# A fused adaLN block, forward and gradients: row loads on POOL's queue, three turns on TensorE, LN and gate work per 128 tokens

## The chip, the core and the metric

The kernel runs on one core of one Trainium2 chip. The metric is device time in microseconds of one execution. Engines are named as in the profile: PE (TensorE matmul), PEld (its weight loads), DVE (VectorE), ACT (ScalarE), POOL (GpSimd), SP (SyncE, here only a queue that issues DMAs).

## The reference

The forward pass is an adaLN-modulated transformer block on one sequence of 2048 tokens, D = 512, 32 heads of 16, and a feed-forward width of 1792 with a squared ReLU. The kernel returns its output and the gradients of nine inputs for a given `grad_out`, all in bfloat16.

```python
mod = (silu(c) @ w_mod).reshape(1, 6, 1, 512)
sa, ca, ga, sb, cb, gb = (mod[:, i] for i in range(6))
h = layernorm(x) * (1 + ca) + sa
q, k, v = split_heads(h @ wqkv)                  # 32 heads of 16
p = softmax(einsum('bhqd,bhkd->bhqk', q, k) * 16 ** -0.5)
x = x + ga * (merge(p @ v) @ wo)
h = layernorm(x) * (1 + cb) + sb
r = relu(h @ w1 + b1)
out = x + gb * ((r * r) @ w2 + b2)
# returned: out and d(out . grad_out)/d(x, wqkv, wo, w1, b1, w2, b2, c, w_mod)
```

## The kernel before

**Four stretches.** A preparation makes LN1, the first keys, queries and values. Then comes the forward attention, with most of the feed-forward and its gradients woven in. Then the last chunk of 512 tokens is finished (`last_chunk`), and then the attention's gradient (the loop over `order_t` and `order_n`) and the final products run. The change touches the second stretch alone.

**Units.** The forward attention is 512 units: 4 query chunks of 512 tokens, in each 8 groups of 4 heads, in each 16 key tiles of 128. For unit u, `fscore(u)` lets PE multiply four heads' keys with the queries (L560, 32 rows of PE for each head) into two PSUM tiles `psST` of two banks, and ACT takes the exponential of each into `ET` (L562). There are three such PSUM tiles, so PE can be about a unit and a half ahead of ACT. `fpv(u - 2)` multiplies `ET` with the values into the one bank `oacc` (L576). After a head group's last tile DVE copies `oacc` to `ostage` (L580), POOL casts it to `obf` (L588), and SP turns it by a DMA transpose into `O_un`.

**What else a unit holds.** All other products of this stretch go through one PSUM bank, the tile `pm` of pool `psM` (function `mm()`, one buffer), so PE can begin the next product only when DVE has copied the last one out. The queues for this work are written by hand:

- `plan` says at which unit the remaining projections of queries, keys and values, token tiles and modulation rows run (`plan_tasks`), and `later_stage` does side jobs every fourth unit: among them LN1's modulated rows `h1_st` (L700 to L703).
- `later(lag, f, ...)` puts a call into `due`, which `run_due` empties at the start of each unit; most DMAs on SP's queue are issued so.
- `dense_chunk(c, O_c, L)` is a generator for one chunk of 512 tokens: the attention's output `O_c` turned to `OT`, the projection with `wo` (L347), LN2, its rows turned to `h2T`, two feed-forward products (L398, L412), LN2's gradient (L434 to L467), the second feed-forward product (L487) and the gradient through `wo` (L519). `step(u)` runs it to its next `yield`; `yield k` makes it wait k further units.
- Products over tokens for the weights' gradients are chains in `dwq` (`add_chain`). Each is four matmuls, a copy by DVE into one of four `part` tiles (L251), and a store to `p_st`: SP's for chunk 0, and for later chunks an accumulating DMA issued by POOL (L255). They run where the generator waits. Chunk 2's chains that are left when the units end run inside `last_chunk` (into `dwbuf`).
- Where a unit has no product, `steady` runs two filler matmuls (L599).

**A chunk's start.** Seven units after a query chunk's last head group, `ffinish` scales its heads (L603) and `chunk_loads(c)` issues the chunk's loads of the gradient, `wo` and x (0.5 MB each) and queues the weights' loads. The last chunk has its own path (`early_finish`, `late_finish`, `last_chunk`).

**What the change touches.** `fload` loads the keys (four transfers of 16 rows x 2048) and queries (four of 16 x 512 and one row of bounds per head, `m_st`) of the next head group, all nine on SP's queue in one unit, at key tile 4 of the group before (tile 10 in the first seven groups). `scaled` multiplies a chunk's gradient by the gate `gb` in one POOL instruction of 128x2048; `sums` adds its four tiles to a row sum. Three turns in `dense_chunk` are DMA transposes from SBUF to SBUF on SP's queue, each followed by a wait of several units:

```python
later(3, sp, OT.rearrange("p t o q -> p (t o) q"), flat(O_c), True)
yield 6
...
later(3, sp, h2T.rearrange("p t o q -> p (t o) q"), flat(xn2_c), True)
yield 6
...
later(5, sp, daT.rearrange("p t o q -> p (t o) q"), flat(da_c), True)
w2_nat = load_wB(w2_src, 1, 0.5)
yield 5
```

Of the kernel before, what the change touches and what calls it, by code (L numbers as in the profile page):

```python
# [15 lines left out]
ALU = mybir.AluOpType  # L16
AX = mybir.AxisListType
BF = dt.bfloat16
F32 = dt.float32

P = 128
D = 512
DC = 4
# [11 lines left out]
def kernel(  # L35
# [8 lines left out]
    TT = n // P  # L44
# [102 lines left out]
    with ExitStack() as ph:  # L147
# [142 lines left out]
        def chunk_loads(c):  # L290
            ts = slice(4 * c, 4 * c + 4)
            end = c == QC - 1
            if end:
                L = dict(begun)
            else:
                L = {"w1": load_wA(w1_src, 6), "w1T": load_wB(w1T_st[:], 20)}
                L["g"] = cb.tile([P, 4, D], BF, name="g_c", tag="g_c")
                sp(L["g"][:], g_dram[:, ts, :])
            L["wo"] = ffw.tile([P, DC, D], BF, name="wo_nat", tag="wo")
            sp(L["wo"][:], A_wo.rearrange("(oc p) j -> p oc j", p=P))  # L300
            L["x1"] = cb.tile([P, 4, D], BF, name="x1_c", tag="x1_c")
            sp(L["x1"][:], x_dram[:, ts, :])
            L["gf"] = cb.tile([P, 4, D], BF, name="gf_c", tag="gf")
            L["gfT"] = cb.tile([P, 4, DC, P], BF, name="gfT", tag="gfT")

            def scaled():
                POOL.tensor_tensor(L["gf"][:], L["g"][:], gb_bc.unsqueeze(1).to_broadcast([P, 4, D]), ALU.mult)
                later(6, sp, L["gfT"].rearrange("p t o q -> p (t o) q"), flat(L["gf"]), True)

            def sums():  # L310
                for ti in range(4):
                    rowsum(4, L["g"][:, ti, :], 4 * c + ti)

            if end:
                return L
            later(5, scaled)
            later(16, sums)
            return L

        def dense_chunk(c, O_c, L):  # L320
# [16 lines left out]
            def normed(ti):  # L337
                t = 4 * c + ti
                DVE.tensor_scalar(xn2_c[:, ti, :], x1_c[:, ti, :], mv4[:, ti, 0:1], rstd2[:, t:t + 1], ALU.subtract, ALU.mult)

            OT = cb.tile([P, 4, DC, P], BF, name="OT", tag="T4")
            later(3, sp, OT.rearrange("p t o q -> p (t o) q"), flat(O_c), True)
            yield 6
            for ti in range(4):
                pa = mm()
                for oc in range(DC):
# [9 lines left out]
            rsqrt_cols(wk, rstd2[:, ts], mv4[:, :, 1], 4)  # L356
            for ti in range(4):
                normed(ti)
            later(3, sp, h2T.rearrange("p t o q -> p (t o) q"), flat(xn2_c), True)
            yield 6  # L360
            while dwq and dwq[0][1] < c:
                yield -2
            for ic in range(DC):
                DVE.tensor_scalar(h2T[:, :, ic, :], h2T[:, :, ic, :],
                                  modcol[:, 4, ic:ic + 1], modcol[:, 3, ic:ic + 1], ALU.mult, ALU.add)
                if ic == 1:
                    yield 0

            def h2_tokens():
                while dwq and dwq[0][1] < c:  # L370
# [105 lines left out]
            dwq[0:0] = chains  # L476
            later(5, sp, dx1_st[:, ts, :], dx1_c)
            daT = cb.tile([P, 4, DC, P], BF, name="daT", tag="T4")
            later(5, sp, daT.rearrange("p t o q -> p (t o) q"), flat(da_c), True)

            w2_nat = load_wB(w2_src, 1, 0.5)
            yield 5
            for ti in range(4):
                t = 4 * c + ti
                pf = mm()
# [58 lines left out]
        def fload(qc, hg):  # L544
            i = hg % 2
            kt_sb, qt_sb = kts[i], qts[i]
            load_rows(kt_sb, qkT_st[1], hg, slice(0, n))
            load_rows(qt_sb, qkT_st[0], hg, slice(512 * qc, 512 * qc + 512), m_st)
            fh[qc, hg] = (qt_sb, kt_sb)

        def fscore(u):
# [113 lines left out]
        def later_stage(i):  # L665
            if i < 4:
                vT = tmpT[:, 4 * (i % 2):4 * (i % 2) + 4, :].rearrange("p a q -> p (a q)")
                sp(vT[:, 0:n], v_st[:, i * P:(i + 1) * P], True)
                later(3, sp, vT_st[i * P:(i + 1) * P, :], vT[:, 0:n])
                return  # L670
            if i < 8:
                ic = i - 4
                nat = tmpT[:, 0:2, :]
                sp(nat, A_wqkv[ic * P:(ic + 1) * P, D:].rearrange("p (t d) -> p t d", t=2))
                nat = nat.rearrange("p t (g d) -> p t g d", d=DH)
                vkp = tmpT[:, 8:10, :].rearrange("p a (g v d) -> p (a g) v d", v=2, d=DH)
                POOL.tensor_copy(vkp[:, :, 1, :], nat[:, 0])
                POOL.tensor_copy(vkp[:, :, 0, :], nat[:, 1])
                later(3, sp, wpad_st[ic * P:(ic + 1) * P, :], tmpT[:, 8:10, :].rearrange("p a q -> p (a q)"))
                return  # L680
            if i < 14:
                for j in (2 * (i - 8), 2 * (i - 8) + 1):
                    wT = tmpT[:, j % 8, :]
                    src = A_wqkv[:, j * P:(j + 1) * P] if j < 4 else wpad_st[:, (j - 4) * P:(j - 3) * P]
                    sp(wT, src, True)
                    later(3, sp, wT_st[j], wT)
                return
            if i >= 26:
                return
            if i == 25:  # L690
                for r, j in enumerate((1, 4)):
                    DVE.reciprocal(racc[0:1, r, :], modbc[0:1, j, :])
                later(3, sp, rows_st[6:8, :].unsqueeze(0), racc[0:1, 0:2, :])
                return
            if i in (18, 20, 21, 24):
                g = (18, 20, 21, 24).index(i)
                hr = tmpT[:, 4 * (g % 3):4 * (g % 3) + 4, :]
                for ti in range(4):
                    t = 4 * g + ti
                    DVE.tensor_scalar(hr[:, ti, :], hr[:, ti, :], mean1[:, t:t + 1], rstd1[:, t:t + 1], ALU.subtract, ALU.mult)  # L700
                DVE.tensor_tensor(hr, hr, ca1_bc.unsqueeze(1).to_broadcast([P, 4, D]), ALU.mult)
                DVE.tensor_tensor(hr, hr, sa_bc.unsqueeze(1).to_broadcast([P, 4, D]), ALU.add)
                later(3, sp, h1_st[:, 4 * g:4 * g + 4, :], hr)  # L703
            if i in (14, 15, 16, 22):
                g = (14, 15, 16, 22).index(i)
                sp(tmpT[:, 4 * (g % 3):4 * (g % 3) + 4, :], x_dram[:, 4 * g:4 * g + 4, :])
# [263 lines left out]
        def plan_tasks():  # L970
            R, T = {}, {}

            def at(u, f, *args):
                plan.setdefault(u, []).append((f, args))
# [51 lines left out]
                later(1, sp, m_st[h0:h1, chunk_cols(g)], mrow[h0:h1, :])  # L1026
                yield

            def query_bound(u, g, hbs, rate):
# [5 lines left out]
                for i in range(6):  # L1035
                    at(u + 1 + i // rate, lambda: next(R["g"]))

            def b1_turn():
                pb = pools["mm"].tile([P, 2 * 512], BF, name="pb1", tag="pm")
# [35 lines left out]
            for g in range(QC):  # L1075
# [6 lines left out]
                at(81 + g, token_tile, 0, 3, g)  # L1082
                for ti in range(4):
                    at(85 + 4 * g + ti, token_tile, 1, g, ti)
            query_bound(21, 0, (1,), 2)
            at(22, b1_turn)
            query_bound(41, 0, (2, 3), 1)
            query_bound(50, 1, (0, 1, 2, 3), 1)
            query_bound(66, 2, (0, 1, 2, 3), 1)
            query_bound(80, 3, (0, 1, 2, 3), 1)  # L1090
# [41 lines left out]
        stages = [*range(4, 14), *range(4), 30, 31, *range(14, 26)]  # L1132
        with ExitStack() as ph2:
            pools["s"] = ph2.enter_context(tc.tile_pool(name="psS", bufs=3, space=bass.MemoryType.PSUM))
            pools["o"] = ph2.enter_context(tc.tile_pool(name="psO", bufs=1, space=bass.MemoryType.PSUM))
# [1 line left out]
            with tc.manual_schedule(engines={PE.engine, ACT.engine, DVE.engine, SP.engine, POOL.engine}):  # L1137
                fh[0, 0] = (qts[0], kts[0])
                for u in range(NF + 2):
                    unit[0] = u  # L1140
                    run_due()
                    if u < NF:
                        if funits[u][2] == (10 if u < 7 * TT else 4) and u + TT < NF:
                            fload(*funits[u + TT][0:2])
                        fscore(u)
                    if 2 <= u:
# [858 lines left out]
```

## Time and profile before

| | |
|---|---|
| median of 3 runs | 2506.2 us (2504.3 to 2511.26) |
| the profiled execution, its own time | 2512.69 us |
| its span, first to last instruction | 2510.9 us |
| mean granted TensorE clock | 0.977 |
| ACT busy | 2304.1 us, 92% of the span |
| PE busy | 2336.8 us, 93% |
| DVE busy | 1818.7 us, 72% |
| POOL busy | 348.1 us, 14% |
| DMA, mean rate | 176 GB/s, 442.40 MB |

A line of the profile's groups reads: source line, engine, operation, output tile <- input tiles, shapes, count, busy us, mean ns of one, and then the idle time of the engine just before these instructions and what ended it. Matmul ends are modelled and pipelined, so busy PE is not PE at its peak. In timelines each row is start (us from the span's start), length, engine, line, operation and tiles, count, and in brackets the idle time before it with its releaser. Rows on SPq are DMA issues: their length is the queue's time, not the transfer's.

### The profile page before, as it was taken

The page shows a single profiled execution, that of the slowest core. Times are in us where ns is not written, and L with a number is a line of the kernel's source. Part 1 is how long each engine was busy: PE and PEld are TensorE (multiplying, and loading weights), DVE is VectorE, ACT ScalarE, POOL GpSimd, SP SyncE. Part 2 cuts the span into 40 slices and gives each one's busy share as a digit, 9 for nine tenths or more (in the row PEclk, how much of TensorE's full clock was granted, in tenths as well). Part 3 has the DMA queues.
Part 4 walks back from the last instruction along what each step waited for, and adds up shares of the span by engine and source line. Part 5 has one row for each costly group of instructions (what it writes and reads, how often), then busy time and mean ns, then how long its engine had stood idle before and what let it go on. Part 6 is the DMA issues. An engine that isn't in the chain of part 4 may idle for free.

```text
span 2510.9 us, 49682 instructions
## 1 busy us (share of the span) xinstructions
PE 2336.8 (93%) x18934; PEld 778.5 (31%) x18934; DVE 1818.7 (72%) x2326; ACT 2304.1 (92%) x3563; POOL 348.1 (14%) x373
## 2 busy tenths in 40 slices
PE   8898889989998999999999999999999999999989
PEld 3232223222322332442332323323232332332244
DVE  6555153445435454578999989999999999999965
ACT  7999999999998999638999999999999999999944
POOL 2000000210323142200111101111011110110100
PEclk9999999999999999998999999999999999999999
DMA  4467455356748766979999999999999999999984
GB/s 142 126 173 174 137 131 133 93 160 134 112 85 169 148 121 129 255 227 172 203 197 198 204 204 204 199 201 203 204 199 202 201 206 200 205 201 211 201 252 133
DMA packets 1207477, 442.40 MB, mean 176 GB/s; under 512 B 1083843, under 2 KB 1178497, under 8 KB 1206854
## 3 DMA queue, kind: packets, MB, share of 16 engines
q1 hardware_dynamic: 1179318, 404.37, 81.6%
q0 software_dynamic: 10944, 16.78, 4.8%
q10 hardware_dynamic: 16976, 18.07, 2.8%
q8 instruction: 149, 2.44, 0.4%
q14 instruction: 90, 0.74, 0.1%
HBM read 98.30 MB, written 70.80 MB: 67 GB/s over the span
## 4 chain that ended last, share of the span: by engine, by line
PE 41%; ACT 39%; issue 7%; DVE 7%; DMA 4%; SPq 1%; ACTq 1%; DVEq 0%; POOL 0%; POOLq 0%
ACT E_u L1583 23%; ACT ET L562 12%; PE dqacc L1664 4%; PE psST L560 4%; PE psS_A L1577 3%; PE pm L233 3%; PE accVK L1637 2%; PE oacc L576 2%; PE psS_B L1577 2%; ACT dsT L1743 2%; DMA dsT<-dS_u 2%; PE psS_C L1577 2%; PE pm L398 2%; PE pm L412 2%; PE pdh L1841 2%
## 5 line engine op out<-in xcount | busy, mean ns | idle before, releaser
L1599 DVE TENSOR_TENSOR dS_u<-psD_u,E_u 128x1024 bf16<-128x1024 f32 x1024 | 1185.8, 1218 | 77.3 <-PE psD_u L1597 29.9
L562 ACT ACTIVATE ET<-psST 128x1024 bf16<-128x1024 f32 x1024 | 942.5, 1251 | 27.5 <-PE psST L560 27.2
L1583 ACT ACTIVATE E_u<-psS_A 128x512 bf16<-128x512 f32 x768 | 510.6, 665 | 10.7 <-DMA d_st<-dltT 7.7
L1583 ACT ACTIVATE E_u<-psS_B 128x512 bf16<-128x512 f32 x768 | 503.8, 656 | 12.4 <-DMA dsT<-dS_u 3.3
L1597 PE MATMUL psD_u<-iv,ido 32*128 32x512 bf16 x2048 | 409.3, 388 | 0.2
L560 PE MATMUL psST<-qt_sb,kt_sb 32*128 32x512 bf16 x2048 | 317.5, 389 | 51.6 <-ACT ET L562 46.9
L1583 ACT ACTIVATE E_u<-psS_C 128x512 bf16<-128x512 f32 x512 | 334.5, 653 | 3.4 <-PE psS_B L1577 1.5
L1577 PE MATMUL psS_B<-ik,iq 32*128 32x512 bf16 x768 | 295.6, 385 | 12.4 <-ACT E_u L1583 4.8
L1577 PE MATMUL psS_A<-ik,iq 32*128 32x512 bf16 x768 | 294.1, 383 | 11.4 <-DVE dwlast L237 1.0
L1577 PEld LDWEIGHTS <-iq 32*128 32x128 bf16 x2048 | 130.0, 91 | 315.6 <-issue 299.7
L1637 PE MATMUL accVK<-dS_u,qz 128*32 128x512 bf16 x2048 | 213.2, 390 | 0.5 <-PE psD_u L1597 0.2
L576 PE MATMUL oacc<-ET,vaug 128*32 128x512 bf16 x2048 | 208.2, 397 | 1.9 <-DVE ostage L580 1.9
L1646 PE MATMUL accVK<-E_u,dOs_tok 128*16 128x512 bf16 x2048 | 204.6, 388 | 0.0
L1682 POOL TENSOR_TENSOR dQacc<-dQacc,dqtmp 128x512 f32<-128x512 f32 x64 | 81.2, 1269 | 857.7 <-ACT dqtmp L1677 857.7
L1577 PE MATMUL psS_C<-ik,iq 32*128 32x512 bf16 x512 | 194.4, 380 | 4.7 <-ACT dqtmp L1677 0.2
L560 PEld LDWEIGHTS <-kt_sb 32*128 32x128 bf16 x2048 | 85.7, 91 | 342.1 <-issue 321.5
L1664 PE MATMUL dqacc<-dsT,KS_tok 128*32 128x512 bf16 x2048 | 147.3, 386 | 19.2 <-DMA dsT<-dS_u 4.9
L1743 ACT ACTIVATE dsT<-ptT 128x1024 bf16<-128x1024 bf16 x128 | 144.8, 1131 | 11.5 <-PE ptT L1627 10.7
L251 DVE COPY part<-pm 128x512 f32<-128x512 f32 (+2 forms) x103 | 63.5, 616 | 119.9 <-PE pm L233 108.2
L1597 PEld LDWEIGHTS <-ido 32*128 32x128 bf16 x2048 | 104.4, 91 | 99.5 <-issue 93.5
L1637 PEld LDWEIGHTS <-qz 128*32 128x32 bf16 x2048 | 58.5, 94 | 178.0 <-issue 162.9
L576 PEld LDWEIGHTS <-vaug 128*32 128x32 bf16 x2048 | 53.1, 93 | 121.7 <-issue 121.7
(404 smaller groups left out, 2517.2 us busy)
## 6 DMA issues: line engine op xcount, KB each, us to landing
p_st<-part POOLq DMA_DIRECT2D x36, 256.0 KB, 5.1
kt_sb<-qkT_st SPq DMA_DIRECT2D x124, 64.0 KB
wA<-in_B_w_dram SPq DMA_DIRECT2D x28, 256.0 KB
wB<-w1T_st SPq DMA_DIRECT2D x21, 256.0 KB
wA<-w2T_st SPq DMA_DIRECT2D x21, 256.0 KB
wB<-in_B_w_dram SPq DMA_DIRECT2D x21, 256.0 KB
p_st<-part POOLq DMA_DIRECT2D x25, 192.0 KB, 4.7
p_st<-part SPq DMA_DIRECT2D x18, 256.0 KB
```

Source lines behind the costliest of these rows:

```text
L560: PE.matmul(ps[:, hi, :], kt_sb[r:r + 32, kt * P:(kt + 1) * P], qt_sb[r:r + 32, :], start=True, stop=True, tile_position=(r, 0))
L562: ACT.activation(ET[:, 2 * pair:2 * pair + 2, :], ps[:], AF.Exp, scale=SCALE)
L576: PE.matmul(oacc[32 * hq:32 * hq + 32, :], lhsT, ET[:, hq, :], start=(kt == 0), stop=(kt == TT - 1), tile_position=(0, 32 * hq), skip_grou ...
L1577: PE.matmul(psS[:], st["q"][r:r + 32, qt * P:(qt + 1) * P], st["k"][r:r + 32, kc * 512:kc * 512 + 512], start=True, stop=True, tile_positi ...
L1583: ACT.activation(bst[u][0][:, hq, :], sst.pop((u, hq))[:], AF.Exp, scale=SCALE)
L1597: PE.matmul(psD[:, hi, :], st["do"][r:r + 32, qt * P:(qt + 1) * P], st["v"][r:r + 32, kc * 512:kc * 512 + 512], start=True, stop=True, til ...
L1599: DVE.tensor_tensor(dS_u[:, 2 * pair:2 * pair + 2, :], psD[:], E_u[:, 2 * pair:2 * pair + 2, :], ALU.mult)
L1637: PE.matmul(cur["vk"][32 * hq:32 * hq + 32, :], hst[hg]["qz"][:, qt, hq, :], bst[u][1][:, hq, :], start=(qt == 0), stop=False, tile_positi ...
L1646: PE.matmul(acc[32 * hq:32 * hq + DH, :], dOs_tok[:, qt, (hg * 4 + hq) * DH:(hg * 4 + hq + 1) * DH], E_u[:, hq, :], start=False, stop=(qt ...
L1664: PE.matmul(acc[32 * hq:32 * hq + 32, :], KS_tok[:, kc * 4 + kt, h * DH:h * DH + 32], tT[:, :, hq * 4 + kt, :], start=(kt == 0), stop=(kt ...
L1682: POOL.tensor_tensor(dst2, dst, tmp[:], ALU.add)
L1743: ACT.activation(dst, pt[:], AF.Identity)
```

## The change

- `fload` puts the nine row loads of a head group on POOL's queue, one in each of nine successive units from key tile 4 on (from the first group on).
- `turned(half, src)` transposes two 128-token tiles by eight PE transposes into the `pm` bank; DVE copies `OT` and `daT` out of it, and for `h2T` applies the modulation on the way out. The waits around the turns change: 6, 6 and 5 units become 2, 2 and 2, with a unit for each half, and two further units after daT's second half.
- The gate's product runs on POOL per 128 tokens in four successive units; its row sums come one in every second unit from 24 units after the loads on, instead of four together after 16.
- LN1's rows for `h1_st` are done per 128 tokens in four successive units. Two reciprocals of 1x512 move from side stage 25 (unit 110) to units 130 and 132.
- The first query bound's steps come slightly earlier (`after` lists the units).

```diff
-            def scaled():
-                POOL.tensor_tensor(L["gf"][:], L["g"][:], gb_bc.unsqueeze(1).to_broadcast([P, 4, D]), ALU.mult)
-                later(6, sp, L["gfT"].rearrange("p t o q -> p (t o) q"), flat(L["gf"]), True)
+            def scaled(ti):
+                POOL.tensor_tensor(L["gf"][:, ti, :], L["g"][:, ti, :], gb_bc, ALU.mult)
+                if ti < 3:
+                    return
+                later(3, sp, L["gfT"].rearrange("p t o q -> p (t o) q"), flat(L["gf"]), True)
...
-            later(5, scaled)
-            later(16, sums)
+            for ti in range(4):
+                later(5 + ti, scaled, ti)
+                later(24 + 2 * ti, sums, ti)
...
+            def turned(half, src):
+                products[0] += 1
+                pt = pools["mm"].tile([P, 2, DC, P], BF, name="ptC", tag="pm")
+                for k in range(2):
+                    for oc in range(DC):
+                        PE.transpose(pt[:, k, oc, :], src[:, 2 * half + k, oc * P:(oc + 1) * P], identb[:])
+                return pt
+
             OT = cb.tile([P, 4, DC, P], BF, name="OT", tag="T4")
-            later(3, sp, OT.rearrange("p t o q -> p (t o) q"), flat(O_c), True)
-            yield 6
+            yield 2
+            for half in range(2):
+                DVE.tensor_copy(OT[:, 2 * half:2 * half + 2], turned(half, O_c)[:])
+                yield 0
...
-            later(3, sp, h2T.rearrange("p t o q -> p (t o) q"), flat(xn2_c), True)
-            yield 6
+            yield 2
             while dwq and dwq[0][1] < c:
                 yield -2
-            for ic in range(DC):
-                DVE.tensor_scalar(h2T[:, :, ic, :], h2T[:, :, ic, :],
-                                  modcol[:, 4, ic:ic + 1], modcol[:, 3, ic:ic + 1], ALU.mult, ALU.add)
-                if ic == 1:
-                    yield 0
+            for half in range(2):
+                pt = turned(half, xn2_c)
+                for ic in range(DC):
+                    DVE.tensor_scalar(h2T[:, 2 * half:2 * half + 2, ic, :], pt[:, :, ic, :],
+                                      modcol[:, 4, ic:ic + 1], modcol[:, 3, ic:ic + 1], ALU.mult, ALU.add)
+                yield 0
...
-            later(5, sp, daT.rearrange("p t o q -> p (t o) q"), flat(da_c), True)
-
             w2_nat = load_wB(w2_src, 1, 0.5)
-            yield 5
+            yield 2
+            for half in range(2):
+                DVE.tensor_copy(daT[:, 2 * half:2 * half + 2], turned(half, da_c)[:])
+                yield 2 * half
...
-            load_rows(kt_sb, qkT_st[1], hg, slice(0, n))
-            load_rows(qt_sb, qkT_st[0], hg, slice(512 * qc, 512 * qc + 512), m_st)
+            rows = list(row_loads(kt_sb, qkT_st[1], hg, slice(0, n)))
+            rows += row_loads(qt_sb, qkT_st[0], hg, slice(512 * qc, 512 * qc + 512), m_st)
+            for i, (to, fro) in enumerate(rows):
+                later(i, POOL.dma_start, to, fro)
+            run_due()
...
-                for ti in range(4):
-                    t = 4 * g + ti
-                    DVE.tensor_scalar(hr[:, ti, :], hr[:, ti, :], mean1[:, t:t + 1], rstd1[:, t:t + 1], ALU.subtract, ALU.mult)
-                DVE.tensor_tensor(hr, hr, ca1_bc.unsqueeze(1).to_broadcast([P, 4, D]), ALU.mult)
-                DVE.tensor_tensor(hr, hr, sa_bc.unsqueeze(1).to_broadcast([P, 4, D]), ALU.add)
-                later(3, sp, h1_st[:, 4 * g:4 * g + 4, :], hr)
+
+                def modulated(ti, t):
+                    DVE.tensor_scalar(hr[:, ti, :], hr[:, ti, :], mean1[:, t:t + 1], rstd1[:, t:t + 1], ALU.subtract, ALU.mult)
+                    DVE.tensor_tensor(hr[:, ti, :], hr[:, ti, :], ca1_bc, ALU.mult)
+                    DVE.tensor_tensor(hr[:, ti, :], hr[:, ti, :], sa_bc, ALU.add)
+
+                for ti in range(4):
+                    later(1 + ti, modulated, ti, 4 * g + ti)
+                later(6, sp, h1_st[:, 4 * g:4 * g + 4, :], hr)
...
-            query_bound(21, 0, (1,), 2)
+            query_bound(21, 0, (1,), (1, 1, 1, 2, 2, 3))
...
+            for r, j in enumerate((1, 4)):
+                at(130 + 2 * r, DVE.reciprocal, racc[0:1, r, :], modbc[0:1, j, :])
+            at(134, sp, rows_st[6:8, :].unsqueeze(0), racc[0:1, 0:2, :])
...
-                        if funits[u][2] == (10 if u < 7 * TT else 4) and u + TT < NF:
+                        if funits[u][2] == 4 and u + TT < NF:
```

More of the change, by code (lines that the diff above doesn't have):

```diff
@@ L304, in chunk_loads, with sums @@
             L["gfT"] = cb.tile([P, 4, DC, P], BF, name="gfT", tag="gfT")
-            def scaled():
-                POOL.tensor_tensor(L["gf"][:], L["g"][:], gb_bc.unsqueeze(1).to_broadcast([P, 4, D]), ALU.mult)
-                later(6, sp, L["gfT"].rearrange("p t o q -> p (t o) q"), flat(L["gf"]), True)
-            def sums():
-                for ti in range(4):
-                    rowsum(4, L["g"][:, ti, :], 4 * c + ti)
+            def scaled(ti):
[3 more added lines that the diff above has]
+                later(3, sp, L["gfT"].rearrange("p t o q -> p (t o) q"), flat(L["gf"]), True)
+            def sums(ti):
+                rowsum(4, L["g"][:, ti, :], 4 * c + ti)
             if end:
                 return L
-            later(5, scaled)
-            later(16, sums)
+            for ti in range(4):
+                later(5 + ti, scaled, ti)
+                later(24 + 2 * ti, sums, ti)
             return L
@@ L689, in later_stage @@
                 return
[L690 to L694, printed above, removed]
             if i in (18, 20, 21, 24):
@@ L1027, in bound, with query_bound @@
                 yield
-            def query_bound(u, g, hbs, rate):
+            def query_bound(u, g, hbs, after):
                 def begin():
@@ L1034, in query_bound @@
                 at(u, begin)
-                for i in range(6):
-                    at(u + 1 + i // rate, lambda: next(R["g"]))
+                for i in after:
+                    at(u + i, lambda: next(R["g"]))
             def b1_turn():
@@ L1084, in plan_tasks @@
                     at(85 + 4 * g + ti, token_tile, 1, g, ti)
-            query_bound(21, 0, (1,), 2)
+            query_bound(21, 0, (1,), (1, 1, 1, 2, 2, 3))
             at(22, b1_turn)
[L1087 to L1090, printed above, removed]
+            query_bound(41, 0, (2, 3), range(1, 7))
+            query_bound(50, 1, (0, 1, 2, 3), range(1, 7))
+            query_bound(66, 2, (0, 1, 2, 3), range(1, 7))
+            query_bound(80, 3, (0, 1, 2, 3), range(1, 7))
+            for r, j in enumerate((1, 4)):
+                at(130 + 2 * r, DVE.reciprocal, racc[0:1, r, :], modbc[0:1, j, :])
+            at(134, sp, rows_st[6:8, :].unsqueeze(0), racc[0:1, 0:2, :])
             for j in range(3):
@@ L1131 @@
         plan_tasks()
-        stages = [*range(4, 14), *range(4), 30, 31, *range(14, 26)]
+        stages = [*range(4, 14), *range(4), 30, 31, *range(14, 25)]
         with ExitStack() as ph2:
```

## The prediction

> **What bounds the kernel now.** First the page, then the stretches by stage.
>
> ```profile
> span 2510.9 us, 49682 instructions
> ...
> L562 ACT ACTIVATE ET<-psST 128x1024 bf16<-128x1024 f32 x1024 | 942.5, 1251 | 27.5 <-PE psST L560 27.2
> ```
> ```profile
> 42.00:1009.00 967.00, 871.60 (x5950) 277.17 (x5946) 453.72 (x883) 942.88 (x1025) 171.97 (x202) 0.98 0.60 135
> 1009.00:1127.00 118.00, 112.50 (x655) 54.58 (x651) 79.50 (x181) 52.86 (x96) 14.43 (x29) 0.99 0.89 244
> ```
>
> The columns after the stretch's length are busy PE, PEld, DVE, ACT and POOL. The forward (42 to 1009) is 512 units; ACT's exponentials fill 942.5 of its 967 us, 1.84 us a unit, while DVE is busy 47% and POOL 18%. So only ACT's idle time can be won there. The next 118 us (the last chunk) are PE's: 112.5 busy. From 1127 on the code is unchanged.
>
> So I read every idle piece of ACT in the forward, in its timeline (start, length, what, idle before):
>
> ```profile
> 200.02 1.94 ACT L562 ACTIVATE ET<-psST 128x1024 bf16<-128x1024 f32 x2 [2.27 <-PE psST L560]
> ...
> 538.09 3.86 ACT L562 ACTIVATE ET<-psST 128x1024 bf16<-128x1024 f32 x4 [2.36 <-PE psST L560]
> ...
> 726.51 1.94 ACT L562 ACTIVATE ET<-psST 128x1024 bf16<-128x1024 f32 x2 [3.02 <-PE psST L560]
> ...
> 799.66 1.94 ACT L562 ACTIVATE ET<-psST 128x1024 bf16<-128x1024 f32 x2 [3.41 <-PE psST L560]
> ...
> 808.76 187.48 ACT L562 ACTIVATE ET<-psST 128x1024 bf16<-128x1024 f32 x204 [2.35 <-PE psST L560]
> ```
>
> With the small ones the pieces add to 23.7 us (without the first, 3.46, where the stage begins): that is the ceiling in the forward. What held PE in each, from the timelines of all engines:
>
> ```profile
> 195.18 1.23 DVE L701 TENSOR_TENSOR tmpT<-tmpT,modbc 128x2048 bf16<-128x2048 bf16 x1
> ```
> ```profile
> 536.31 0.56 DVE L251 COPY part<-pm 128x384 f32<-128x384 f32 x1 [3.05 <-DMA p_st<-part]
> ```
> ```profile
> 714.87 2.85 SPq L178 DMA_DIRECT2D wB<-in_B_w_dram  x5
> 717.82 0.49 SPq L178 DMA_DIRECT2D dx_st<-dx_c  x1
> 718.40 8.25 SPq L178 DMA_TRANSPOSE daT<-a_c  x1
> ...
> 724.86 1.01 PE L487 MATMUL pm<-wB,sT 128*128 128x512 bf16 x2 [2.39 <-DMA wB<-in_B_w_dram]
> ```
> ```profile
> 795.96 0.42 DVE L251 COPY part<-pm 128x256 f32<-128x256 f32 x1 [6.18 <-DMA p_st<-part]
> ...
> 797.13 1.89 PE L347 MATMUL pm<-wo_nat,OT 128*128 128x512 bf16 x4 [2.86 <-DMA OT<-O_c]
> ...
> 804.48 1.26 DVE L330 TENSOR_TENSOR x_c<-atmp,x_c 128x512 bf16<-128x512 bf16 x1
> ```
>
> A block on DVE, a late store, a late weight load, a late transpose: each stops PE at its one "pm" bank, and ACT a little later. How much later is PE's lead: at 195 DVE held LN work for about 4.05 us (1.6 for four L700 at 0.40, 1.23, 1.22) and ACT lost 2.27, so the lead is about 1.8 us, one unit.
>
> **The change, part by part** (us of ACT's idle time taken away).
>
> *LN rows per 128 tokens.* The bursts cost 2.27 and 0.42 at 200 to 202, and 0.68 and 0.71 at 216 and 224: 4.08. Now each unit gets one L700 (0.40) and two 128x512 products (0.42 each, from L401's 42 alike): 1.25 us. Where token copies (0.42) and the bound (0.67) fall into the same unit DVE has 2.34 us for 1.84, four times: 2.0 us behind, against 1.8 of lead. I leave 0.5: gain 3.6. The two reciprocals (3.3 us each) move to units 130 and 132, which hold no dense work: nothing. The bound's step pulled forward a unit: nothing to 0.4, counted nothing.
>
> *Row loads off SP.* The queue held them from 708.30 to 714.82, 6.5 us, ahead of five of w2's seven loads, and just before the p_st store that DVE waited for at 536. The store goes out when its unit comes: 2.36 and the 0.56 behind it, 2.9 gained. For w2 the daT transpose (8.25 us on SP, beside the landing) also goes, and w2's first use moves from 6 units after the loads to 7. The waits from 726 to 735 (3.02, 0.56, 1.44, 0.63) are 5.65: gain 5.6. Cover gone, the wB loads are late again and all 5.65 returns.
>
> *OT, h2T and daT by TensorE.* Each adds 16 transposes per chunk, 144 in all; eight take 0.72 us (L1276), where a unit without a product ran two fillers of 0.59 (L599): PE is not nearer to its limit. Eviction of OT and daT halves is 128x1024; the nearest row is 128x768 in 0.56 (L629), so about 0.70, twelve of them. For h2T, eight pieces of 128x256 from PSUM at 0.41 (L1283) replace four of 0.41: 1.64 more a chunk. Spread over units, DVE's half-idle time hides them; uncovered they cost 12 x 0.70 + 3 x 1.64 = 13 us. What goes is OT's wait before 799.66, 3.41. But see what is late next: DVE's copy waited for p_st until 795.96, 1.2 us before OT came, and that bank is what the transposes need. Between 1.2 and 3.4; the row nearest to it is that copy: 1.2.
>
> *Gate and row sums per 128 tokens.* At 803 DVE's products took 1.26 and 1.37 instead of 0.42 beside POOL's four row sums (4.96 us): 0.98 and 2.35 of idle time. The sums move to 24 units after the chunk's loads; but the gate's four pieces (4.38 / 4 = 1.1 us) now fall on those units. In chunk 2 the four output projections stand in successive units with 2.40 us of DVE each (0.69 + 0.42 + 0.42 + 0.69 + 0.18), 2.2 behind even without POOL. Between none and all of 3.33: I take half, 1.7. The pieces at 318 and 558 (1.72) are alike: 0.9.
>
> *Fewer units per chunk.* The waits before OT and h2T shrink by more than daT's grow (some 4 units a chunk). In the changed program eight of chunk 2's chains stand behind the forward instead of eleven; one of 384 columns takes PE 0.65 us there, and PE is the bound: 3 x 0.65 = 2.0 gained.
>
> *Added waits.* 279 row loads join POOL's in-order queue at 0.87 us each (L255's median): nine a head, 7.8 us of 29.4. Behind them stand accumulating stores, row sums, db1's additions and obf; PE waits for the last row, m_st, due 4 units (7.4 us) after its issue. The row nearest is POOL's p_st issue, 3.4/5.2/13.2 us to landing: 0.87 + 5.2 = 6.1, in time. At 785 to 800, where a chunk's 1.5 MB of loads run, the median landing was 9.2: 10.1 against 7.4 + 1.8, 0.9 late. Between 0 and 15 for three chunk starts (13.2 + 0.9 - 9.2 = 4.9 at each); taken: 2. The p_st wait itself can move to PE's new work; between 0 and 6.2 (its row), taken 3.1.
>
> The page "SBUF — State Buffer" of the Trainium skill, section "Who interferes with whom", speaks against this part: a DMA issued from GpSimd is starved of its descriptor writes while VectorE is in a two-port mode, and should go to SP's or ACT's queue. So far the trace does not bear it out: 65 issues of L255 to p_st from part took 0.85 to 1.22 us with DVE at work. What slower issues would do is a rival below.
>
> Sum: 3.6 + 2.9 + 5.6 + 1.2 + 1.7 + 0.9 + 2.0 = 17.9, less 5.1: 12.8 us. The profiled execution took 2512.69 us (span 2510.9, 1.8 around it), 6.5 above the median of three, 2506.2 (2504.3 to 2511.26). Its own sum gives 2499.9; carried to the median: **2493.5 us**. A measurement of this kernel can tell about 0.3% (7.5 us) from no change.
>
> **The rivals.**
>
> *All of it goes.* PE's bank is free at every chunk start, rows land in 5 us: 23.7 less the 0.18, 0.18, 0.94 and 1.34 of pieces that no edit touches, plus 2.0: 23.1 us, 2483. For it: every large piece has its own edit. Against: the 6.18 us wait of DVE for p_st.
>
> *The waits change their names.* Chunk starts stay crowded: OT 0, gate and sums 0, added waits 9 (6.2 and 2.8); 3.6 + 2.9 + 5.6 + 2.0 - 9 = 5.1: 2501, no change that can be told. For it: the four projections overfill DVE anyhow. A variant is that the profiled execution's waits are its own (it was 6.5 slower than the median), with about the same time.
>
> *POOL's rows come late: slower.* One mechanism, at chunks 1 and 2 (15 heads), where POOL's ring also carries accumulating stores. A landing of 13.2 us makes m_st 4.9 us late for ACT. From three such heads on the 12.8 us are gone; with five, 24.5 - 12.8 = 11.7 slower, 2518. For it: one ring in order, and landings over 9.2 at 785 to 800. Against: medians of 4.0 to 5.3 in the other stretches.
>
> *It isn't on the path.* If w2 and the p_st store are late from traffic rather than order, only 3.6 + 2.0 remains: 2501.
>
> *POOL issues slowly.* If DVE's work holds up each row's issue for as long as the slowest POOL issue of the trace (2.06 us, to p_st from dwbuf), nine rows take 18.5 of a head's 29.4 us; only chunk starts are late, 9.2 + 2.06 - 9.2 = 2.1 at each, 6.2 in place of 2: 8.6 gained, 2497.6. For it: nothing yet but that one row. It is the case of the Trainium skill's page "SBUF — State Buffer" (section "Who interferes with whom").
>
> **How the numbers follow.** Forecast 0.49, all of it 0.16, slow issue 0.03, changed names 0.13, off the path 0.05, late rows 0.14. The first three are faster by over 0.3% (below 2498.7): 0.68. The two at 2501 make same 0.18; late rows, slower 0.14. The range goes from the full gain, 2483, to 2508: it takes in both cases near no change and the start of the late rows, and leaves about 0.1 above and as much below, for a lead over 1.8 us or a store that waits less.
>
> **What would show it.** Right: ACT's idle time before L562 falls from 27 to about 15 us, with no piece near 726 and 538; E_u begins about 13 us earlier; eight chains behind the forward; p_st landings at a chunk's start under 9 us. Wrong: PE waiting for kt_sb or qt_sb; DVE copies waiting for p_st over 6 us at more than one chunk; POOL issues well over 0.9 us; idle pieces at the units of ptC.

## The result and the profile after

The changed kernel takes 2489.9 us in the median (2479.6 to 2504.2) where the kernel before, beside it, takes 2504.4. The two medians make a ratio of 0.9942; the estimate over all runs, which is used below, is 0.9958 (95% interval 0.9939 to 0.9977), 0.4% faster. In a second measurement the ratio is 0.9945 (0.9923 to 0.9967). The forecast, 2493.5 of 2506.2, is a ratio of 0.9949.

The profiled execution took 2503.09 us (span 2501.3); before it was 2512.69. Here are the lines of the page, and the two stretches in the columns of before (busy PE, PEld, DVE, ACT, POOL):

```profile
span 2501.3 us, 49888 instructions
...
L578 ACT ACTIVATE ET<-psST 128x1024 bf16<-128x1024 f32 x1024 | 941.9, 1242 | 16.6 <-PE psST L576 16.3
```

```profile
41.00:997.00 956.00, 860.80 (x5998) 283.45 (x6061) 473.58 (x935) 942.67 (x1025) 312.96 (x490) 0.99 0.58 132
997.00:1116.00 119.00, 110.56 (x629) 52.34 (x639) 78.70 (x181) 51.97 (x94) 12.40 (x26) 0.99 0.87 239
```

ACT's own work in the forward is what it was (942.9 to 942.7 us). Its idle time fell from 27.2 to 16.3 us (23.7 to 12.8 without the first piece), and the forward, first to last exponential, from 966.5 to 955.0. The last phase, from there to the first `E_u`, did not shorten: 118.9 before, 119.4 after, although PE has about 2 us less work in it. So the gain is the forward's, 11.4 us. From the first `E_u` on the code is the same in all versions, and that stretch took between 1366.8 and 1386.6 us in the fourteen profiles shown below; so single profiles are compared here by stage, and whole times by the ratios.

The pieces of ACT's idle time near 200 to 224, 538, 726 to 735 and 808 are gone. What is left that is long stands in chunk 2 (ACT's timeline, idle time in brackets):

```profile
768.11 15.10 ACT L578 ACTIVATE ET<-psST 128x1024 bf16<-128x1024 f32 x16 [3.35 <-PE psST L576]
...
796.74 1.94 ACT L578 ACTIVATE ET<-psST 128x1024 bf16<-128x1024 f32 x2 [2.55 <-PE psST L576]
799.23 4.69 ACT L578 ACTIVATE ET<-psST 128x1024 bf16<-128x1024 f32 x5 [0.55 <-PE psST L576]
```

PE's list of waits (total, times, longest) names what held it there, and a third wait in the last phase:

```profile
PE ptC L348 <- DVE xn_c L341: 3.3, 2, 2.9
...
PE pm L674 <- DVE part L251: 2.8, 2, 2.3
PE pc L233 <- ACT tk L1323: 2.3, 4, 1.2
```

The first is the turn of h2T: it comes three units after LN2's last vector work is queued, and DVE is still at it. Part of this is the change's own doing. One of the row sums that it moved now runs beside LN2, and a vector instruction on 128x4 elements, which takes 0.16 us elsewhere in the same sequence, ends only with it:

```profile
791.60 1.97 DVE L127 TENSOR_TENSOR rsq<-rsq 128x4 f32<-128x4 f32 x1
```

```profile
792.37 1.17 POOL L170 TENSOR_TENSOR racc<-racc,g_c 128x512 f32<-128x512 f32 x1
```

This instruction takes 1.97 or 1.98 us in the five profiles in which that row sum falls there (changed, changed again, chain lag, w1 later, rows later), and in no version with separate sums where the sum falls elsewhere: with the rows back on SP it runs at 787.2, and the two pieces after it are 1.03 and 0.84 us instead of 2.55 and 0.55.

The second of PE's waits is for the `part` copies, which wait for `p_st`. The third does not occur before: PE waits for ACT's copies of turned sT tiles.

POOL's row loads (name, count, shortest/median/longest in ns):

```profile
L188 POOL DMA_DIRECT2D qt_sb<-qkT_st x124: 484/484/832, 55.8 to 956.2; - x124
L188 POOL DMA_DIRECT2D qt_sb<-m_st x31: 552/575/876, 63.2 to 956.7; - x31
```

They issue in 0.48 or 0.58 us in the median, not 0.87, and no score waits for its rows in this profile.

### The profile page after: what moved, and what is told of

Its sections match the earlier page's. It is cut to its first block, busy times and chain, and to the rows that moved or that the text cites. A ratio compares the mean times of both kernels' runs of the same rounds, so it can differ in the third digit from the quotient of the medians.

```text
span 2501.3 us, 49888 instructions
## 1 busy us (share of the span) xinstructions
PE 2324.0 (93%) x18948; PEld 783.4 (31%) x19036; DVE 1837.7 (73%) x2377; ACT 2303.7 (92%) x3560; POOL 488.0 (20%) x661
## 4 chain that ended last, share of the span: by engine, by line
ACT 40%; PE 38%; issue 8%; DVE 7%; DMA 3%; SPq 1%; ACTq 1%; POOL 0%; DVEq 0%; another core or an unknown queue 0%; POOLq 0%
ACT E_u L1600 24%; ACT ET L578 12%; PE dqacc L1681 4%; PE psST L576 3%; PE psS_A L1594 3%; PE accVK L1654 2%; PE pm L233 2%; ACT dsT L1760 2%; PE psS_B L1594 2%; PE pdh L1858 2%; PE oacc L592 2%; PE psS_C L1594 2%; PE pwq L1892 2%; PE pm L500 2%; PE pm L410 2%
## 5 line engine op out<-in xcount | busy, mean ns | idle before, releaser
L578 ACT ACTIVATE ET<-psST 128x1024 bf16<-128x1024 f32 x1024 | 941.9, 1242 | 16.6 <-PE psST L576 16.3
L1760 ACT ACTIVATE dsT<-ptT 128x1024 bf16<-128x1024 bf16 x128 | 144.1, 1126 | 13.1 <-PE ptT L1644 12.2
L251 DVE COPY part<-pm 128x512 f32<-128x512 f32 (+2 forms) x106 | 65.2, 615 | 121.9 <-PE pm L233 111.8
L1699 POOL TENSOR_TENSOR dQst<-dQacc,dqtmp 128x512 bf16<-128x512 f32 x32 | 40.6, 1270 | 266.1 <-ACT dqtmp L1694 266.1
```

The lines of the kernel that those rows point to most:

```text
L578: ACT.activation(ET[:, 2 * pair:2 * pair + 2, :], ps[:], AF.Exp, scale=SCALE)
L1699: POOL.tensor_tensor(dst2, dst, tmp[:], ALU.add)
L1760: ACT.activation(dst, pt[:], AF.Identity)
```

## The experiments

Each ratio is to the kernel before on the same chip. Lengths are those of one profiled execution each, in us. ACT's idle time is the sum of its gaps over 0.15 us before the exponentials, without the first piece.

| kernel | forward | ACT idle in it | last phase | ratio (95%) |
|---|---|---|---|---|
| before | 966.5 | 23.7 | 118.9 | 1 |
| changed | 955.0 | 12.8 | 119.4 | 0.9958 (0.9939 to 0.9977) |
| changed, again | 954.5 | 12.4 | 118.7 | 0.9945 (0.9923 to 0.9967) |
| rows back on SP | 959.4 | 17.7 | 121.9 | 1.0003 (0.9987 to 1.0020) |
| DMA turns | 955.5 | 13.6 | 118.5 | 0.9965 (0.9946 to 0.9984) |
| blocks whole | 968.4 | 23.7 | 119.3 | 1.0017 (1.0001 to 1.0034) |
| gate and sums whole | 961.1 | 17.9 | 119.9 | 0.9988 (0.9969 to 1.0006) |
| before + rows on POOL | 969.4 | 26.0 | 118.4 | 1.0015 (0.9996 to 1.0035) |
| chain lag | 954.0 | 10.9 | 116.7 | 0.9931 (0.9906 to 0.9955) |
| more units | 947.6 | 6.2 | 125.7 | 0.9931 (0.9906 to 0.9956) |
| w1 later | 956.1 | 13.2 | 121.0 | 0.9950 (0.9931 to 0.9969) |
| turn and lag | 957.5 | 15.2 | 117.7 | 0.9978 (0.9962 to 0.9995) |
| gate later | 963.5 | 19.2 | 118.0 | 0.9982 (0.9969 to 0.9995) |
| rows later | 1027.3 | 80.7 | 121.2 | 1.0231 (1.0204 to 1.0259) |

### One part undone

**Rows back on SP.**

```diff
-            rows = list(row_loads(kt_sb, qkT_st[1], hg, slice(0, n)))
-            rows += row_loads(qt_sb, qkT_st[0], hg, slice(512 * qc, 512 * qc + 512), m_st)
-            for i, (to, fro) in enumerate(rows):
-                later(i, POOL.dma_start, to, fro)
-            run_due()
+            load_rows(kt_sb, qkT_st[1], hg, slice(0, n))
+            load_rows(qt_sb, qkT_st[0], hg, slice(512 * qc, 512 * qc + 512), m_st)
...
-                        if funits[u][2] == 4 and u + TT < NF:
+                        if funits[u][2] == (10 if u < 7 * TT else 4) and u + TT < NF:
```

> The changed kernel with its row loads back on SP's queue, nine at once as in the kernel before; all else changed. After: forward (first to last exponential) 955.05 us, ACT idle before its line 12.8 us without the first piece. Theory (the rows' place in SP's queue held the p_st store and the w2 loads): the piece near 538 is back (2.4 + 0.6), and of the w2 pieces near 726 (5.65) about half, since daT's transpose no longer stands in the queue: forward about 960.8, time about 5.7 us above the changed kernel. Rival A (the rows on POOL pay for it with the p_st wait near 768): that piece of 3.35 goes, net +2.4, forward 957.4. Rival B (traffic, not the order in the queue, made those late): no piece near 538 or 726, forward 955, no change.

By the times the whole gain is gone (1.0003), but not where it was looked for: 532 has 0.83, 726 has nothing. One piece of 8.2 us near 844 takes their place. SP's queue and PE there:

```profile
827.41 1.80 SPq L140 DMA_DIRECT2D qt_sb<-qkT_st  x4
829.25 0.54 SPq L140 DMA_DIRECT2D qt_sb<-m_st  x1
829.90 3.22 SPq L178 DMA_TRANSPOSE tk<-sT  x2
833.21 8.92 SPq L178 DMA_DIRECT2D wA<-w2T_st  x7
```

```profile
841.52 1.89 PE L424 MATMUL pm<-gfT,wA 128*128 128x512 bf16 x4 [7.66 <-DMA wA<-w2T_st]
```

The rows, from 824.5 to 829.8, stand ahead of two turns and of w2T's loads. Chunk 1's loads of w2 went out at 685.8, well ahead of the rows at 699.1; it is chunk 2's w2T that the rows hold now. What nine rows on SP delay is whatever the chunk loads at that moment; the theory's mechanism holds, its place and size do not. The profile does not account for the whole loss: the forward gives back 4.3 of its 11.4 us, and the last phase is 2.5 us longer, where PE waited 3.5 us for `tk` and not for rows.

**DMA turns.** OT, h2T and daT go back to SP's transposes with `yield 6`, `yield 6` and `yield 5`, as in the kernel before (the removed lines of the diff above, put back).

> The changed kernel with OT, h2T and daT turned by SP's DMA transposes again, with the waits of 6, 6 and 5 units; all else changed. Theory (the turns bring little: the wait of 2.55 + 0.55 before h2T's turn eats what OT's turn won): OT's wait near 800 is back at 1.2 to 3.4, h2T's 3.1 goes, w2 comes back late by at most 2: forward 954 to 957, no difference that can be measured; eleven chains stand behind the forward again. Rival (turning by TensorE is what made w2 come in time): pieces near 726 of 5.65 and OT's 3.41 are back, forward about 961.

The forward is 955.5, no different: beside the rest of the change, the turns by TensorE bring nothing that can be told. The pieces are others, though. Two of 2.5 us, near 723 and 935, are late rows; the first in PE's timeline:

```profile
722.87 0.40 PE L573 MATMUL psST<-qt_sb,kt_sb 32*128 32x512 bf16 x4 [2.77 <-DMA qt_sb<-m_st]
```

**Blocks whole.** LN rows, gate and row sums whole again.

```diff
-            for ti in range(4):
-                later(5 + ti, scaled, ti)
-                later(24 + 2 * ti, sums, ti)
+            later(5, scaled)
+            later(16, sums)
...
-                for ti in range(4):
-                    later(1 + ti, modulated, ti, 4 * g + ti)
-                later(6, sp, h1_st[:, 4 * g:4 * g + 4, :], hr)
+                DVE.tensor_tensor(hr, hr, ca1_bc.unsqueeze(1).to_broadcast([P, 4, D]), ALU.mult)
+                DVE.tensor_tensor(hr, hr, sa_bc.unsqueeze(1).to_broadcast([P, 4, D]), ALU.add)
+                later(3, sp, h1_st[:, 4 * g:4 * g + 4, :], hr)
```

> The changed kernel with the LN rows, the gate and the row sums whole again (one block of 128x2048 each, sums 16 units after the chunk's loads); all else changed. Theory: the bursts on DVE cost ACT 4.08 at 200 to 224 again, and the four row sums beside the projections up to 3.33: forward 955.05 + 4.1 + 2.6 = about 961.7. Rival (with rows gone from SP and OT turned early, PE's lead covers them): 4.1 or less, forward at most 957.5.

This costs more than anything else undone, 13.3 us of forward, and twice what the theory said. Six pieces from 201 to 228 are the LN bursts, 5.4 us. Two others had not been seen at this size. DVE, POOL and ACT near 540:

```profile
539.44 6.36 DVE L617 TENSOR_TENSOR O_c<-O_un,r_inv 128x512 bf16<-128x512 bf16 x4
```

```profile
540.57 4.08 POOL L307 TENSOR_TENSOR gf_c<-g_c,modbc 128x2048 bf16<-128x2048 bf16 x1 [16.23 <-DMA g_c<-in_grad_out_dram]
```

```profile
547.83 1.94 ACT L576 ACTIVATE ET<-psST 128x1024 bf16<-128x1024 f32 x2 [3.44 <-PE psST L574]
```

Four scalings of `O_c` take 6.36 us beside POOL's gate and 2.50 where no gate runs (chunk 2). One of the four makes the difference: it takes 4.54 us instead of 0.68, about as long as the gate. In the kernel before the same happens in chunk 0, where ACT lost nothing until 318:

```profile
299.30 6.36 DVE L603 TENSOR_TENSOR O_c<-O_un,r_inv 128x512 bf16<-128x512 bf16 x4
```

The Trainium skill's page "SBUF — State Buffer", section "Who interferes with whom", says that a VectorE instruction with two SBUF inputs contends with a GpSimd instruction that reads SBUF, and that the ports they share are an exclusive lock; this case's trace agrees (0.68 against 4.54 us beside a gate of 4.08). Near 812 the four row sums (4.90 us on POOL) stand beside LN2's small vector instructions, of which four take 1.00 to 1.33 us instead of 0.16, and ACT waits 4.41.

**Gate and sums whole**, LN rows per 128 tokens (the first hunk above alone).

> The changed kernel with only the gate and the row sums whole again (one 128x2048 gate, four sums together at 16 units); the LN rows stay per 128 tokens. With LN rows whole too the forward was 968.4, 13.3 longer than the changed kernel's. Theory: the LN bursts make 4.1 of that (pieces at 201 to 226), the rest is POOL's blocks beside DVE's: forward 954.7 + 9 = 964. Rival (the prediction's sizes: gate and sums 2.6): 957.3.

The forward is 961.1, between theory and rival: 6.1 of the 13.3 us are the gate's and the sums' (6.6 against the changed kernel's second profile), with pieces of 3.44 near 539 and 3.26 near 804. The other 7.3 go with the LN rows, of which the pieces from 201 to 228 show 5.4.

### One part alone

**Before + rows on POOL** (the rows' hunk of the change, in the kernel before).

> The kernel before with the row loads on POOL's queue, one per unit, and nothing else of the change. Before: forward 966.5 us. Theory: the p_st store's 2.9 goes, and about half of w2's 5.65, since daT's transpose (8.25 us on SP) still stands ahead of them: forward 960.8, 5.7 us below the kernel before. Rival A (the rows alone held w2): 8.5 gained, forward 958. Rival B (rows on POOL come late or delay POOL's accumulating stores at chunk starts): 3 or more given back, forward 963.8 or longer.

The length is Rival B's. The p_st piece at 538 and the w2 pieces (2.92 and 5.65) are gone as the prediction has it, and all of it is given back: 4.04 and 2.41 near 735 and 949, where m_st comes late, and 3.63 near 546, where the gate now meets `O_c` (6.36 us again), which is no part of Rival B. The late rows in POOL's and PE's timelines:

```profile
728.70 0.49 POOL L188 DMA_DIRECT2D qt_sb<-qkT_st  x1 [6.88 <-DMA p_st<-part]
```

```profile
734.75 0.62 PE L563 MATMUL psST<-qt_sb,kt_sb 32*128 32x512 bf16 x4 [4.09 <-DMA qt_sb<-m_st]
```

A row load's issue stood still for 6.88 us until an accumulating store had landed, and m_st, issued behind it at 729.18, let PE go 5.6 us later. The run with the DMA turns shows the same at 717.2 (5.99 us). This is the prediction's slower rival at work in kind: the rows come late behind POOL's other work.

### The margin of the rows

**Rows later**: begun at key tile 7 instead of 4.

```diff
-                        if funits[u][2] == 4 and u + TT < NF:
+                        if funits[u][2] == 7 and u + TT < NF:
```

> The changed kernel with each head's nine row loads begun at its seventh unit instead of its fourth, so that the last, m_st, is issued one unit before the next head's first score instead of four (5.5 us less). It prices the rival in which POOL's rows come late. Theory (landing of m_st at a median of 3.3 us and a lead of PE of 1.8 us): about 0.5 + 3.3 - 1.84 = 2 us late against 1.8 of lead, so most heads lose under 0.5 us; those at three chunk starts, with landings of 9.8, lose up to 6.7 - 1.8 = 5 each: forward 955 + 6 to 20. Rival (POOL runs ahead of the units and issues its rows as soon as the one before is out, so the order by units hardly matters): forward 955 to 957.

Three units, 5.5 us, cost 72 us of forward, far over the theory's 20. From PE's waits:

```profile
PE psST L576 <- DMA qt_sb<-m_st: 28.3, 9, 6.4
PE psST L576 <- issue: 21.5, 5, 5.3
```

Twelve head changes lose 2.8 to 5.6 us each. Landing is not slower than in the changed kernel (3.6 against 3.2 us in the median for m_st). But POOL is in order: at 694.9, for one, m_st goes out behind a store and row sums that had waited 4.23 us for DVE. So it comes later than its unit, and the margin of three units is what covers that.

### Is it one execution's own?

**Changed, again**, without an edit.

> The changed kernel once more, for a second profile of it beside the others of this call: forward 955 us, pieces of ACT's idle time again near 768 (3.35) and 797 (2.55 + 0.55), last phase (end of the forward to the first E_u) 119.4 us. Rival: those pieces are one execution's own, and this profile has others; then differences of 3 us or less between single profiles decide nothing.

The idle time in sum is nearly the same, 12.4 against 12.8 us; its places move. 768 has 1.14 instead of 3.35, while 312, 536 and 551 have 1.74, 1.49 and 1.73 where the first profile had 0.45 at two of them. Near 536 `O_c` takes 4.41 us here beside the gate's pieces, which POOL runs in one go:

```profile
530.66 5.42 POOL L307 TENSOR_TENSOR gf_c<-g_c,modbc 128x512 bf16<-128x512 bf16 x4 [16.21 <-DMA g_c<-in_grad_out_dram]
```

`later(5 + ti, ...)` gives them four units, but POOL waits for no unit. They run once `g_c` has landed and POOL comes to them.

### The last phase

**Chain lag.**

```diff
-                    dwq.append(add_chain(c, 1, fc, D, lambda ti: tk[:, f, ti, :], lambda ti: gf_c[:, ti, :],
+                    dwq.append(add_chain(c, 2, fc, D, lambda ti: tk[:, f, ti, :], lambda ti: gf_c[:, ti, :],
```

> The changed kernel with one edit in the last chunk: a chain on a turned part of sT may start two ticks after its turn instead of one. Theory (with only eight chains of chunk 2 left, PE runs out of chains and waits for ACT's copy of the turned tile: 0.24 + 1.20 + 0.35 + 0.48 = 2.3 us): those waits go, last phase 117.1 us instead of 119.4, 2.3 us less in all. Rival (ACT or DVE bound the last phase, PE's waits are only where it shows): phase 119 or longer.

The theory: the waits for `tk` are gone, and the phase is 116.7 instead of 118.7 and 119.4. In the median it takes 2484.1 us, against 2488.8 for the changed kernel and 2504.9 for the kernel before beside it. The intervals of the two ratios overlap; that it beats the changed kernel rests on the phase, in one profile.

**More units.**

```diff
-            yield 2
+            yield 4
             while dwq and dwq[0][1] < c:
...
-                yield int(c < QC - 2 and ti < 3)
+                yield int(ti < 3)
```

> The changed kernel with more units where it waits: four instead of two ahead of h2T's turn in every chunk, and one unit between chunk 2's four output projections, as chunks 0 and 1 have. Theory: the pieces at 797 and 799 (3.1) and the three at 784 to 789 (1.5) go, forward about 950.5; thirteen chains stand behind the forward instead of eight, which fill PE's waits for the turned tiles first: 5 x 0.65 - 2.3 = 1 us more there, 120.4; in all 3.5 us less than the changed kernel. Rival (PE's one bank is late for other reasons, p_st at the chunk's start): the wait is only moved, forward 954 or longer.

The forward is better than expected, 947.6, with 6.2 us of idle time. The last phase takes all of it, 125.7 instead of 120.4. By the code, a thirteenth chain needs a part slot that the loads of the stored parts already use, so some partial sums of the output `out_4` are overwritten and that output is wrong; the time is read only for where it goes. ACT waits there for such a load, and PE 3.9 us for ACT:

```profile
1033.85 0.60 ACT L1323 ACTIVATE tk<-ptk 128x512 bf16<-128x512 bf16 x1 [6.29 <-DMA part<-p_st]
```

**Turn and lag**: `yield 4` ahead of the turn and the lag, without the units between the projections.

> The changed kernel with four units instead of two ahead of h2T's turn, and the last chunk's two-tick lag (both tried in the call before, the first together with another edit). Ten chains then stand behind the forward. Theory: the two pieces near 797 (2.0 + 0.8) go, forward 951.6; two more chains of 0.65 make the last phase 116.7 + 1.3 = 118.0; in sum 1.5 us less than with the lag alone (2484.1): 2482.6. Rival (each unit added to chunk 2 comes back whole in the last phase, as thirteen chains cost 7 us there): phase 119.5, no gain over the lag alone.

The last phase is as computed, 117.7. The forward is not: 957.5, with 3.83 near 797. The units were filled with chains, whose copies stand behind the same vector work (DVE, then PE):

```profile
793.27 1.38 DVE L341 TENSOR_SCALAR xn_c<-x_c,mv,rstd 128x512 bf16<-128x512 bf16 x4
794.56 0.42 DVE L251 COPY part<-pm 128x256 f32<-128x256 f32 x1
```

```profile
795.03 1.01 PE L233 MATMUL pm<-tk,h_c 128*128 128x256 bf16 x4 [4.15 <-DVE part L251]
```

So the piece near 797 is not a matter of how early the turn comes. LN2's 16 small instructions and four rows hold DVE from 790.3 to 794.6, here without a row sum beside them, and whatever holds PE's one bank meanwhile waits. In the forward this run lacks only the units between chunk 2's projections that the run with more units had, and there the piece was gone; so, by one profile of each, it is those units, ahead of LN2, that took it away. Two more pieces (2.09 near 879, 1.31 near 915) are not explained.

### Two that missed

**w1 later**: `load_wA(w1_src, 12)` in place of 6.

> The changed kernel with the seven loads of w1 queued six units later (12 after the chunk's loads instead of 6). Theory (w1's 1.8 MB, which SP issues at the chunk's start, make the p_st stores land in 6 to 9 us, and DVE's copies wait for them): the piece near 768 (3.35) falls under 1, forward about 952, unless w1 now comes late for the first product near 801. Rival (the accumulating stores are slow by themselves, or the row loads on POOL's queue delay them): the piece stays at 3 or more.

It decides nothing: the piece is 1.26 here, but 1.14 and 1.30 in two profiles without the edit (changed again, chain lag). What makes the stores to `p_st` near 757 land in 8.2 and 9.3 us in the changed kernel's first profile and in 7.5 at most in its second stays open.

**Gate later**: the gate's pieces at `later(26 + ti, ...)`, the sums at `later(33 + 2 * ti, ...)`, on top of turn and lag.

> As the kernel with turn and lag, and the gate's four pieces stand 26 to 29 units after the chunk's loads instead of 5 to 8 (behind a copy to obf that waits for DVE's ostage), the row sums from 33 on. Theory (POOL keeps no units: its gate pieces start together when g_c has landed, and beside them DVE's four O_c scalings take 4.2 to 4.4 us instead of 2.50): O_c takes 2.5 us in all three chunks, the piece near 536 (1.49) goes, forward 950. Rival (the stretch only moves: the gate now runs beside the projections' or the MLP's vector work): O_c 2.5, but forward unchanged or longer than with turn and lag alone.

`O_c` takes 2.50 us in all three chunks, so the collision is understood; but the forward is 6 us longer than without the edit. The rival has the number; that the gate now disturbs other vector work is not shown. The largest new piece, 2.17 near 772, stands behind a `part` copy that waited 2.86 us for `p_st`. Others at 353, 466, 852 and 885 came in, whose causes were not followed.

## Why the prediction was right, point by point

**What bounds the kernel.** Right. ACT's work stayed at 942.7 us and the gain is idle time taken away, 10.9 us of the 23.7. `E_u` begins 11.8 us earlier; 13 was said. One of the signs named for a wrong forecast did appear, idle pieces at the units of `ptC`.

**LN rows, +3.6.** Right to a little low: all pieces, 4.08, are gone, and undoing the rows as well as the gate costs 7.3.

**Rows off SP, +2.9 and +5.6.** The pieces went as said, also where the rows alone were moved (before + rows on POOL). But the term stands on one alignment of heads and chunks: with rows on SP and the rest changed, the loss comes at 844 on w2T, and its size, 4.3 us of forward, is not the 8.5 that was said.

**Turns, +1.2.** Small as said, and that by luck. OT's 3.41 went. What was counted as hidden, h2T's turn, brought 2.55 + 0.55 (2.02 + 0.83 in the second profile): three units after the vector work it finds DVE busy, where the step looked at DVE's mean load and not at the block of LN2 just ahead. About 1.8 us of that block are the instruction held beside the row sum, which the step on the sums had not foreseen either. Undoing all three turns costs 0.5.

**Gate and row sums, +2.6.** The term that was too small: undone, 6.1 to 6.6. The step priced the pieces seen at 802 to 808 and 318 and 558, but not what the same gate does when it falls fully on `O_c`, though a row of 6.36 us for that stood in the profile of before (299.30, where it cost ACT nothing that can be seen).

**Fewer chains, +2.0.** Wrong. Eight chains stand behind the forward, as said, and the phase did not shorten. The step took PE as the bound at 112.5 busy of 118. The chains were also what PE did while ACT copied the turned tiles; without them it waits 2.3 us. With the lag the 2.0 appear: 116.7 instead of 118.9.

**Added waits, -5.1.** The p_st wait at a chunk's start was taken as 3.1; the piece behind it is 3.35 in the first profile and 1.14 in the second (a store landed in 9.3 us in the first, where under 9 was named as a sign of being right). Late rows were taken as 2: nothing. The issue was priced at 0.87 us and takes 0.48.

Forward and last phase together, then, gained 10.9 us in the first profile and 12.2 in the second, against 12.8 forecast: gate and sums gave more, the chains nothing, and that these cancel is luck.

**The rivals.** *POOL's rows come late* was the dangerous one. It did not happen in the changed kernel, but it did, with 5.7 and 6.8 us of PE's waiting, in two versions that lack a part of the change, and 72 us with three units less. It had the queue in order right, but priced slow landings (13.2 us). Where rows came late, their landing was ordinary (3.6 us in the median with three units less); it was their issue that stood behind a store or a row sum. *POOL issues slowly*: no. All 279 issues took 0.48 to 1.16 us with DVE 50% busy. By the Trainium skill's page "SBUF — State Buffer", section "Who interferes with whom", a DMA issued from GpSimd is starved while VectorE is in a two-port mode; in the twelve profiles with rows on POOL the longest issue of a row took 1.5 us, so it was never held for long. *It isn't on the path*: no. Rows moved alone take both pieces away, and rows back on SP bring the ratio to 1.0003. *The waits change their names* describes single parts (DMA turns; rows alone), not the whole.

## What to carry to other kernels

A hand-written lag orders a queue; it holds nothing back on an engine that waits for no unit. Where a block on GpSimd must not meet vector work, ask what it really waits for. Work that is left over for a later, busy stage may be the cover of a wait there: before counting its removal as a gain, look at what the bounding engine does in its place. And parts of a change that each move the alignment of two periodic loops (heads and chunks) can't be priced one by one from one profile: in their profiles, the rows alone made the forward 3 us longer, and without the split blocks the rest brought nothing.

## What was not expected of the hardware

- In the median POOL issues a copy of 16 rows in 0.48 us and one of four rows in 0.58; an accumulating store of 128 rows takes 0.87.
- After PE had stood still for 7.7 us (841.5, rows on SP) and for 2.7 us (949.4, before + rows on POOL), the next four 128x512 matmuls took 1.89 us instead of 1.04. It is not so each time: with the DMA turns they took 1.04 after waits of 2.77 and 2.97 us (722.9 and 934.9). With more units the granted clock was 0.90 in the 25 us after PE's wait of 3.9 us, against 1.00 in the same stretch of the changed kernel. So a wait of PE can cost more than its length.
